# Causal attention and an ELU feed-forward on one core: new durations, and engines counted free ahead of an operation's end, in the plan that orders the instructions

## The chip, the core and the metric

The kernel runs on 1 core of one Trainium2 chip. The metric is device microseconds of one execution. The kernel before was run three times: 1034.64 us in the median, 1034.17 the fastest and 1037.37 the slowest.

## The reference

Eight batches of eight heads, 576 positions, head size 64; the bias of the scores is a cumulative sum along each head. Its output, 4608 tokens of 512, goes through a feed-forward with 2048 hidden units. All inputs are float32 except for the two weight matrices, which come as float64.

```
cum = np.cumsum(np.maximum(s, 0.0), axis=-1)
bias = -(cum[:, :, :, None] - cum[:, :, None, :])
scores = scale * np.matmul(q, k.transpose(0, 1, 3, 2))
scores = np.where(causal, -1000000000.0, scores + np.minimum(bias, 0.0))
attn = softmax(scores)
x = np.matmul(attn, v).transpose(0, 2, 1, 3).reshape(B * S, H * D)
h = x @ w_in
g = np.where(h > 0.0, h, np.exp(np.minimum(h, 0.0)) - 1.0)
return g @ w_out
```

## The kernel before

**Attention.** A unit is one head of one batch, or a pair of heads for the first 64 rows. `prepare` loads keys and queries (tiles stk, stq), rounds them to float32r (kh, qs; helper `rounded`, lines 400 to 410) and takes the rest that rounding left (k, q; helper `rest`, 421 to 427), so that a score is two matmuls: rounded by rounded, and the rests. `softmax_block` (1140 to 1165) makes the scores of a block of 128 rows on TensorE (line 1151, PSUM bank sc), adds the mask and finds the extreme of each row on VectorE (1154, tile mn), and takes the exponent with its sum on ScalarE (1159); 1163 and 1165 make the reciprocals of the sums. `halved` (1178 to 1215) splits the weighted probabilities into two float16 parts, high (1202 on GpSimd, 1204 on VectorE or 1206 on ScalarE) and low (1210 on VectorE, or 1196 and 1197, two instructions, on GpSimd), and a DMA transposes them into T. `weighing` (1262) multiplies them with the values (1324, bank av); `produce` (805) splits the result into the network's float16 input x. The first pairs ("low" units, lines 853 to 995, tiles kl, ql, pl, tl, avl) work in plain float32, with transposes on TensorE (947 and 968).

**Network.** The 4608 tokens are 18 chunks of 256. For each chunk and each pair of hidden blocks, `hidden` (1518) makes 24 float16 matmuls into a bank h (1539), five steps of the ELU on ScalarE and VectorE (1557, 1562 or 1566, 1570, 1574 or 1576, 1579, tiles g and gg), and `project` (1584) makes 2 x 6 matmuls into o (1600). The first chunk, and a part of the second, use float32 matmuls instead (1475 and 1505), because the weights' float16 parts are not ready.

**The plan.** Nothing of this is issued in program order. Each call of `op` registers an operation: a priority, one or more ways to do it (an engine, a cost in ns, a function that issues the instructions), and the tiles read and written. `Plan.issue` (178 to 288) then works like a list scheduler. It keeps a time `free` for each engine. In each step it computes for every operation whose inputs are planned when it could start: the latest of the engine's `free`, the end of its inputs plus a hop between engines (99 to 106), the time its buffers come free plus 150 ns, and, for the ways named DVE-SB and Pool, a port between VectorE and GpSimd, whose user's end less a lead is the other's earliest start. Among an operation's ways it takes the one with the earliest start plus cost, with VectorE's cost taken 1.3-fold (108, 109). It issues the operation with the earliest start, and of equals the one with the lower priority number: the network's steps beside TensorE have -1000, attention 0 to some 300, the network's matmuls 10000 and more. The planned order of each engine is the order in which it runs on the chip, and each engine waits at its next instruction until that one's inputs are there. Some switches go by the planned time of TensorE: the filler transposes (1663, 300 of them on offer) end at 60 us, one PSUM bank goes from the scores to the hidden layer at 165 us, and at 300 us the choice of certain buffers changes.

The costs are functions of the columns n: `pe`, `pe4`, `pe16` for TensorE, `act_c`, `act_s` for ScalarE, `dve_p`, `dve_b`, `dve_1`, `dve_2` for VectorE, `pool_1`, `pool_2` for GpSimd (291 to 341), or numbers in place. An operation can be several instructions.

Of the kernel before, what the change touches and what calls it, by code (L numbers as in the profile page):

```python
# [17 lines left out]
P = 128  # L18
# [70 lines left out]
class Plan:  # L89
# [20 lines left out]

    PORT_LEAD = {"DVE-SB": 240.0, "Pool": 120.0}

    ENGINE = {"DVE-SB": "DVE", "Pool-M": "Pool"}
# [64 lines left out]
    def issue(self):  # L178
# [19 lines left out]
        while pending:  # L198
# [56 lines left out]
            self.log.append((engine, start, end, o.prio))  # L255
            free[engine] = end
            for b, k in o.new:
# [33 lines left out]
def pe(n):  # L291

    return max(0.4525 * n, 111.0)


def pe4(n):

    return 4 * pe(n)

# [36 lines left out]
def pool_1(n):  # L336
    return 120 + 1.04 * n
# [7 lines left out]
def kernel(  # L345
# [66 lines left out]
    def scaled(prio, n, dst, src, by, reads, writes):  # L412

        op(prio, [
            ("Pool", 160 + 1.04 * n,
             lambda: pool.tensor_scalar(dst(), src(), by(), 1.0, ALU.mult, ALU.mult)),
            ("ACT", 295 + n / 1.2, lambda: act.activation(dst(), src(), AF.Copy, scale=by())),
            ("DVE-SB", 220 + 0.7 * n, lambda: dve.tensor_scalar(dst(), src(), by(), None, ALU.mult)),
        ], reads, writes)
# [52 lines left out]
    def clear_keys(k):  # L472

        return [("Pool-M", pool_1(2 * LOW), lambda: pool.memset(k()[HB:], 0.0))]

# [154 lines left out]
    def scales_of(prio, spans, dst):  # L630

        n = len(spans)
        tops = all_tops[n > 1 or dst == S_FIRST]
        bank = any_bank(f"peaks_{dst}")
        every = lambda: bank.v[:, P : P + n]
        own = plan.buf(sb, [P, 4], F32, f"own_{dst}", tag="own_first" if dst == S_FIRST else f"own{n}")

        def largest():
            for m, (at, k) in enumerate(spans):
                dve.tensor_reduce(tops.v[:, m : m + 1], peaks.v[:, at : at + k], mybir.AxisListType.X, ALU.max)  # L640

# [12 lines left out]
        op(prio, [("PE", pe4(P), lambda: pe_.matmul(every(), all_ones.v, own.v[:, :n], start=True, stop=True))],  # L654
           [all_ones, own], [bank])
        op(prio, [("DVE", 160.0, lambda: dve.tensor_copy(scales.v[:, dst : dst + n], every()))],
           [bank], [(scales, dst)])
# [208 lines left out]
    def prepare_low(u):  # L866
# [10 lines left out]
        load(prio, lambda: queries()[:HB], lambda: qT[b, j, :HB, : 2 * LOW], [], [key("q")], P * LOW * 4)  # L877
        op(prio if n else -10, [("Pool-M", pool_1(2 * LOW), lambda: pool.memset(queries()[HB:], 1.0))],
           [], [key("ones")])
# [58 lines left out]
    def weighing_low(u):  # L938
# [6 lines left out]
        def pair():  # L945
            tr = score_bank(f"trl_{u.tag}")
            op(prio, [("PE", 111.0, lambda: pe_.transpose(tr.v[:, :P], u.first.v, ident))], [u.first], [tr],
               late=[low_scale[u.b]] if u.b in low_scale else ())
            psum_copy(prio, P, lambda: turned.v[:, :P], lambda: tr.v[:, :P], [tr], [(turned, "pair")])

            def products():
                for h in range(2):
                    pe_.matmul(av.v[h * HB : (h + 1) * HB, :HB], u.vs_of()[:, 0], turned.v[:, h * HB : (h + 1) * HB],
                               start=True, stop=True)

            op(prio, [("PE", 2 * pe4(HB), products)], [(turned, "pair"), u.vs], [av])

        def keys(kb):
# [27 lines left out]

            op(prio, [("PE", pe4(c), products)], [(turned, kb), u.vs], [av])
            if kb < CUT:
# [151 lines left out]
    def softmax_block(prio, tag, native, pt, w, mask, mv, reads, operands, inv, view=lambda v: v):  # L1140
# [4 lines left out]
        for i in range(n):  # L1145
            sc = score_bank(f"sc_{tag}_{i}")

            def scores(i=i, sc=sc):
# [3 lines left out]

            op(prio, [("PE", pe4(cw) if native else 2 * pe(cw), scores)], reads, [sc])
            op(prio, [("DVE", 84 + dve_p(cw), lambda i=i, sc=sc: dve.tensor_tensor_reduce(  # L1154
                pt.v[:, i * cw : (i + 1) * cw], sc.v[:, :cw], mv(i * cw, cw), scale,
                BIG if i == 0 else mn.v[:, 0:1], ALU.add, ALU.min, mn.v[:, i : i + 1]))],
               [sc, mask], [(pt, "data"), mn])
        sm, col, last, ns, up = inv
        op(prio, [("ACT", 480 + w / 1.2, lambda: act.activation(  # L1159
            pt.v[:, :w], pt.v[:, :w], AF.Exp, bias=mn.v[:, n - 1 : n], scale=-1.0,  # L1160
            accum_out=sm.v[:, col : col + 1]))], [mn], [(pt, "data"), (sm, col)])
        if last:
            op(prio, [("ACT", 225.0, lambda: act.activation(
                sm.v[:, :ns], sm.v[:, :ns], AF.Relu, bias=EPS / up, scale=1.0 / up))], [], [sm])
            op(prio, [("DVE", 180.0, lambda: dve.reciprocal(sm.v[:, :ns], sm.v[:, :ns]))], [], [sm])  # L1165

    def normalize(prio, pt, w, sm, col):
        r = slice(col, col + 1)
        op(prio, [
            ("Pool", 160 + 1.04 * w, lambda: pool.tensor_scalar(  # L1170
                pt.v[:, :w], pt.v[:, :w], sm.v[:, r], 1.0, ALU.mult, ALU.mult)),
# [6 lines left out]
    def halved(u, i, pt, sm, col):  # L1178
# [20 lines left out]
        for part, n in ((whole, k * P), (rest, HB))[: 1 + (i == u.last)]:  # L1199
            high, low = (part, 0), (part, 1)  # L1200
            op(prio, [
                ("Pool", 160 + 1.04 * n, lambda part=part: pool.tensor_scalar(  # L1202
                    part(t16, 0), own(part), sm.v[:, r], 1.0, ALU.mult, ALU.mult)),
# [207 lines left out]
    def input_scale(ch, cs):  # L1411
# [7 lines left out]
        def steps():  # L1419
# [10 lines left out]

        op(side, [("DVE-SB", 80.0 + 160 * (len(cols) - 1), steps)],
           [(scales, c + m) for c in cols for m in range(2)], [(cs, "input")])
        if len(cols) == 1:
            return
        for m, (lo, up, _) in enumerate(parts):
            x, o = xs[lo // TX], lo % TX
            keys = [(part, *key) for a, e, _, key in x_parts[lo // TX] if a < up and e > lo for part in range(2)]
            op(side, [("DVE-SB", 100 + 0.55 * 8 * (up - lo), lambda x=x, o=o, n=up - lo, m=m: dve.tensor_scalar(
                x.v[:, :, :, o : o + n], x.v[:, :, :, o : o + n], cs.v[:, 1 + m : 2 + m], None, ALU.mult))],
               [(cs, "input")], [(x, key) for key in keys])  # L1440

    def group_constants(ch, cs):
# [4 lines left out]
        def steps():  # L1447
# [297 lines left out]
```

## Time and profile before

| | |
|---|---|
| median of three runs | 1034.64 us |
| the profiled execution | 1037.26 us, its span 1035.5 us, granted clock 1.00 |
| PE (TensorE) matmuls | 98% of the span |
| ScalarE (ACT) and GpSimd (POOL) | 616.0 and 418.0 us busy |
| float16 hidden matmuls, L1539 on x | 3072, 377.2 us |
| float16 output matmuls, L1600 | 1608, 380.7 us |
| moved by the DMA queues | 137.76 MB, 133 GB/s over the span |

The span goes from the first to the last instruction. PE stands for matmuls, PEld for weight loads, DVE for VectorE, SP for SyncE, which issues the DMAs. Matmuls are pipelined and their ends are modelled, so the time of a matmul is read best from the start of one to the start of the next. A row of a group gives the line, engine, operation, tiles out<-in, shapes and count, then the busy time and the mean ns of one, then the idle time of the engine just before them and what ended it. A row of waits gives who waited for whom, the us in total, the number of times and the longest.

### The profile page before, as it was taken

What the parts mean: (1) busy time and instruction counts of PE and PEld (TensorE: products, weight loads), DVE (VectorE), ACT (ScalarE), POOL (GpSimd) and SP (SyncE); (2) the same over time, 40 slices, a digit from 0 to 9 for tenths busy, and PEclk for the clock granted to TensorE, in tenths of its full rate; (3) what the DMA queues carried; (4) which work ended last, traced back from release to release, by engine and by line L of the source; (5) the groups of instructions that cost most, each with busy time, mean ns of one, the idle gap of its engine ahead of it and who ended that gap; (6) DMA issues with size and microseconds to landing.
All of it is one profiled execution on the core that took longest, in us unless ns stands there. A gap on an engine that the chain in (4) does not pass through costs nothing.

```text
span 1035.5 us, 21491 instructions
## 1 busy us (share of the span) xinstructions
PE 1010.8 (98%) x7181; PEld 697.0 (67%) x7181; DVE 848.1 (82%) x2119; ACT 616.0 (59%) x1452; POOL 418.0 (40%) x675
## 2 busy tenths in 40 slices
PE   8899999999999999999999999999999999999998
PEld 6666666666666666676666666666767676766665
DVE  6999899898788888888898888888889888884333
ACT  4787755656567556666566656666555555653232
POOL 5342335634445345555555445453343344330000
PEclk9999999999999999999999999999999999999999
DMA  8666356374667655667565866675766556642000
GB/s 207 218 219 197 114 167 133 87 171 104 147 126 151 160 117 119 145 155 173 112 143 121 184 120 144 129 176 117 152 131 165 119 134 133 140 95 52 1 21 21
DMA packets 277823, 137.76 MB, mean 133 GB/s; under 512 B 211768, under 2 KB 255056, under 8 KB 277712
## 3 DMA queue, kind: packets, MB, share of 16 engines
q1 hardware_dynamic: 277712, 136.39, 56.5%
q8 instruction: 57, 0.93, 0.4%
q14 instruction: 54, 0.44, 0.1%
HBM read 70.22 MB, written 9.88 MB: 77 GB/s over the span
## 4 chain that ended last, share of the span: by engine, by line
PE 82%; DVE 9%; DMA 4%; issue 2%; ACT 1%; SPq 1%; POOL 0%; DVEq 0%; POOLq 0%; ACTq 0%
PE o L1600 32%; PE h L1539 30%; PE sc L1151 9%; PE av L1324 6%; DVE p L1210 2%; DMA w_raw<-in_w_out_dram 2%; PE o L1505 1%; DMA vs<-in_vb_dram 1%; PE h L1475 1%; SPq L392 1%; DVE p L1154 1%; PE avl L984 1%; PE trl L968 1%; DMA q<-qs 1%; DVE peaks L616 1%
## 5 line engine op out<-in xcount | busy, mean ns | idle before, releaser
L1600 PE MATMUL o<-wp,gg 128*128 128x512 f16 x1608 | 380.7, 380 | 0.6 <-DVE gg L1579 0.6
L1539 PE MATMUL h<-x,wp 128*128 128x256 f16 x3072 | 377.2, 273 | 1.7 <-DVE gg L1579 1.7
L1539 PEld LDWEIGHTS <-wp 128*128 128x128 f16 x3216 | 301.3, 98 | 68.8 <-issue 9.6
L1600 PEld LDWEIGHTS <-gg 128*128 128x128 f16 x1608 | 150.3, 98 | 155.7 <-issue 6.0
L1159 ACT ACTIVATE p<-p,mn 128x192 f32<-128x192 f32 (+1 forms) x232 | 143.9, 621 | 55.9 <-DVE mn L1154 50.6
L1210 DVE SCALAR_TENSOR_TENSOR p<-p,sm,p 128x512 f16<-128x512 f32 (+3 forms) x240 | 171.8, 739 | 2.9 <-POOL p L1202 1.3
L1557 ACT ACTIVATE g<-h,cs 128x512 f32<-128x512 f32 x134 | 91.8, 685 | 122.9 <-PE h L1539 120.6
L1202 POOL TENSOR_SCALAR p<-p,sm 128x512 f16<-128x512 f32 (+3 forms) x124 | 79.4, 647 | 132.9 <-DVE sm L1165 85.4
L1574 ACT ACTIVATE gg<-h,wc 128x512 f16<-128x512 f32 x125 | 85.7, 685 | 71.6 <-DVE h L1570 70.3
L1154 DVE CUSTOM_DVE_ANT_0 p<-sc,maskw 128x192 f32<-128x192 f32 (+1 forms) x232 | 108.6, 480 | 16.8 <-PE sc L1151 14.8
L1579 DVE SCALAR_TENSOR_TENSOR gg<-h,wc,gg 128x512 f16<-128x512 f32 x134 | 99.8, 745 | 17.7 <-ACT gg L1574 16.9
L1151 PE MATMUL sc<-kh,qs 128*128 128x192 f32 (+2 forms) x272 | 109.8, 407 | 4.3 <-DVE mn L1154 4.1
L1570 DVE SCALAR_TENSOR_TENSOR h<-g,cs,h 128x512 f32<-128x512 f32 x134 | 100.7, 752 | 11.1 <-ACT g L1562 6.8
L1151 PE MATMUL sc<-k,q 128*128 128x192 f32 (+2 forms) x272 | 83.8, 311 | 1.8 <-issue 1.1
L1566 DVE TENSOR_SCALAR g<-g 128x512 f32<-128x512 f32 x76 | 36.1, 475 | 56.0 <-ACT g L1557 55.6
L1151 PEld LDWEIGHTS sc<-kh,qs 128*128 128x128 f32 x272 | 51.5, 189 | 23.1 <-DVE mn L1154 7.9
L1206 ACT ACTIVATE p<-p,sm 128x512 f16<-128x512 f32 (+3 forms) x97 | 55.8, 592 | 14.8 <-DVE sm L1165 13.3
L1324 PE MATMUL av<-T,v 128*64 128x256 f16 (+5 forms) x896 | 60.4, 286 | 0.0
L425 POOL TENSOR_TENSOR qs<-stq,qs 64x512 fp32r<-64x512 f32 (+1 forms) x44 | 49.4, 1122 | 26.4 <-ACT qs L406 11.7
L1151 PEld LDWEIGHTS sc<-k,q 128*128 128x128 f32 x272 | 51.8, 190 | 4.6 <-issue 1.3
L1324 PEld LDWEIGHTS <-v 128*64 128x64 f16 x896 | 39.9, 110 | 19.2 <-issue 8.9
L404 POOL TENSOR_SCALAR qs<-stq 128x512 fp32r<-128x512 f32 (+1 forms) x36 | 19.3, 536 | 79.8 <-PE sc L1151 65.0
(194 smaller groups left out, 1384.2 us busy)
## 6 DMA issues: line engine op xcount, KB each, us to landing
stk<-in_kT_dram SPq DMA_DIRECT2D x64, 288.0 KB
stq<-in_qT_dram SPq DMA_DIRECT2D x40, 256.0 KB
va<-in_vb_dram SPq DMA_DIRECT2D x32, 320.0 KB
w_raw<-in_w_in_dram SPq DMA_DIRECT2D x16, 512.0 KB
w_raw<-in_w_out_dram SPq DMA_DIRECT2D x16, 512.0 KB
out_dram<-ost SPq DMA_DIRECT2D x32, 256.0 KB
q<-qs SPq DMA_DIRECT2D x40, 128.0 KB
T<-p SPq DMA_TRANSPOSE x208
```

Source lines behind the costliest of these rows:

```text
L1151: pe_.matmul(view(sc.v[:, :cw]), l, r, start=n == 0, stop=n == len(pairs) - 1)
L1154: op(prio, [("DVE", 84 + dve_p(cw), lambda i=i, sc=sc: dve.tensor_tensor_reduce(pt.v[:, i * cw : (i + 1) * cw], sc.v[:, :cw], mv(i * cw, c ...
L1159: op(prio, [("ACT", 480 + w / 1.2, lambda: act.activation(pt.v[:, :w], pt.v[:, :w], AF.Exp, bias=mn.v[:, n - 1 : n], scale=-1.0, accum_out ...
L1202: ("Pool", 160 + 1.04 * n, lambda part=part: pool.tensor_scalar(part(t16, 0), own(part), sm.v[:, r], 1.0, ALU.mult, ALU.mult)),
L1210: ("DVE-SB", dve_2(n), lambda part=part: dve.scalar_tensor_tensor(part(t16, 1), own(part), sm.v[:, r], part(t16, 0), ALU.mult, ALU.subtract)),
L1324: pe_.matmul(av.v[w.h * HB : (w.h + 1) * HB, dst], w.values.v[:, w.h, kb, v], part(w, kb, m), start=n == 0, stop=n == len(order) - 1,)
L1539: pe_.matmul(hp.v[:, m], weight_part(f, 0, part)[1]()[:, c * P : (c + 1) * P], x.v[:, xx, c, o : o + TC], start=(c == 0 and i == 0), stop= ...
L1557: op(side, [("ACT", act_c(2 * TC) + 90, lambda: act.activation(gt.v, flat(hp.v), AF.Exp, scale=by(BACK)))], [hp, (cs[ch], g)], [gt])
L1570: op(side, [("DVE", dve_b(2 * TC), lambda: dve.scalar_tensor_tensor(flat(hp.v), gt.v, by(MINUS if sign[0] else FIRST), flat(hp.v), ALU.mul ...
L1574: ("ACT", act_c(2 * TC) + 90, lambda: act.activation(flat(gg.v[:, 0]), flat(hp.v), AF.Copy, scale=down())),
L1579: op(side, [("DVE", dve_b(2 * TC), lambda: dve.scalar_tensor_tensor(flat(gg.v[:, 1]), flat(hp.v), down(), flat(gg.v[:, 0]), ALU.mult, ALU. ...
L1600: pe_.matmul(acc[i].v, gg.v[:, a, m, i * P : (i + 1) * P], weight_part(2 * fp + m, 1, part)[1](), start=(first and m == 0 and k == 0), sto ...
```

## The change

Three things change, all of them in numbers that the plan uses; no instruction, tile or dependency does.

First, after an operation is planned, its engine is counted free 85 ns (VectorE) or 105 ns (ScalarE) ahead of the operation's end; those who read its result still wait for the end. Second, TensorE's costs: float32 matmuls go from 1.81 n to 1.675 n + 5 ns; the products of two heads, each on half of the array's columns, get a cost of their own, and a score of two float32r matmuls gets 85 ns more. Third, single costs of the other engines: the masked score 74 ns less, the exponent 90 ns less, GpSimd's scaling 235 + 0.9 n in place of 160 + 1.04 n, GpSimd's way for the low halves 420 ns more, its wide memsets less, and some runs of small steps on VectorE more.

```
+    OVERLAP = {"DVE": 85.0, "ACT": 105.0}
...
-            free[engine] = end
+            free[engine] = end - self.OVERLAP.get(engine, 0.0)
...
 def pe4(n):
-    return 4 * pe(n)
+    return 1.675 * n + 5
+def pe4_half(n):
+    return 200 + 1.1 * n
+def pe_score(n):
+    return 2 * pe(n) + 85
...
     scaled, normalize, halved (high):
-            ("Pool", 160 + 1.04 * n,
+            ("Pool", 235 + 0.9 * n,
...
     memsets of low units' keys and queries:
-        return [("Pool-M", pool_1(2 * LOW), lambda: pool.memset(k()[HB:], 0.0))]
+        return [("Pool-M", 120 + 0.72 * 2 * LOW, lambda: pool.memset(k()[HB:], 0.0))]
...
     scales_of:
-        op(prio, [("DVE", 600.0, exponents)], [bank], [own])
-        op(prio, [("PE", pe4(P), ...
+        op(prio, [("DVE", 840.0, exponents)], [bank], [own])
+        op(prio, [("PE", 145.0, ...
...
     weighing_low:
-            op(prio, [("PE", 2 * pe4(HB), products)], [(turned, "pair"), u.vs], [av])
+            op(prio, [("PE", pe4_half(HB), products)], [(turned, "pair"), u.vs], [av])
-            op(prio, [("PE", pe4(c), products)], [(turned, kb), u.vs], [av])
+            op(prio, [("PE", pe4_half(c), products)], [(turned, kb), u.vs], [av])
...
     softmax_block:
-            op(prio, [("PE", pe4(cw) if native else 2 * pe(cw), scores)], reads, [sc])
-            op(prio, [("DVE", 84 + dve_p(cw), ...
+            op(prio, [("PE", pe4(cw) if native else pe_score(cw), scores)], reads, [sc])
+            op(prio, [("DVE", 10 + dve_p(cw), ...
-        op(prio, [("ACT", 480 + w / 1.2, ...
+        op(prio, [("ACT", 390 + w / 1.2, ...
-            op(prio, [("ACT", 225.0, ...
-            op(prio, [("DVE", 180.0, ...
+            op(prio, [("ACT", 205.0, ...
+            op(prio, [("DVE", 170.0, ...
...
     halved (low):
-                ("Pool", pool_1(n) + pool_2(n), lambda part=part: scaled_rest(part)),
+                ("Pool", 420 + pool_1(n) + pool_2(n), lambda part=part: scaled_rest(part)),
...
     input_scale, group_constants:
-        op(side, [("DVE-SB", 80.0 + 160 * (len(cols) - 1), steps)],
+        op(side, [("DVE-SB", 80.0 + 360 * (len(cols) - 1), steps)],
-            op(side, [("DVE-SB", 100 + 0.55 * 8 * (up - lo), ...
+            op(side, [("DVE-SB", 100 + 0.27 * 8 * (up - lo), ...
-        op(-1000 + ch, [("DVE-SB", 450.0, steps)],
+        op(-1000 + ch, [("DVE-SB", 780.0, steps)],
```

More of the change, by code (lines that the diff above doesn't have):

```diff
@@ L652, in scales_of @@
            [tops], [bank])
-        op(prio, [("DVE", 600.0, exponents)], [bank], [own])
-        op(prio, [("PE", pe4(P), lambda: pe_.matmul(every(), all_ones.v, own.v[:, :n], start=True, stop=True))],
+        op(prio, [("DVE", 840.0, exponents)], [bank], [own])
+        op(prio, [("PE", 145.0, lambda: pe_.matmul(every(), all_ones.v, own.v[:, :n], start=True, stop=True))],
            [all_ones, own], [bank])
@@ L877, in prepare_low @@
         load(prio, lambda: queries()[:HB], lambda: qT[b, j, :HB, : 2 * LOW], [], [key("q")], P * LOW * 4)
-        op(prio if n else -10, [("Pool-M", pool_1(2 * LOW), lambda: pool.memset(queries()[HB:], 1.0))],
+        op(prio if n else -10, [("Pool-M", 120 + 0.72 * 2 * LOW, lambda: pool.memset(queries()[HB:], 1.0))],
            [], [key("ones")])
@@ L1151, in scores @@
                     pe_.matmul(view(sc.v[:, :cw]), l, r, start=n == 0, stop=n == len(pairs) - 1)
-            op(prio, [("PE", pe4(cw) if native else 2 * pe(cw), scores)], reads, [sc])
-            op(prio, [("DVE", 84 + dve_p(cw), lambda i=i, sc=sc: dve.tensor_tensor_reduce(
+            op(prio, [("PE", pe4(cw) if native else pe_score(cw), scores)], reads, [sc])
+            op(prio, [("DVE", 10 + dve_p(cw), lambda i=i, sc=sc: dve.tensor_tensor_reduce(
                 pt.v[:, i * cw : (i + 1) * cw], sc.v[:, :cw], mv(i * cw, cw), scale,
@@ L1158, in softmax_block @@
         sm, col, last, ns, up = inv
-        op(prio, [("ACT", 480 + w / 1.2, lambda: act.activation(
+        op(prio, [("ACT", 390 + w / 1.2, lambda: act.activation(
             pt.v[:, :w], pt.v[:, :w], AF.Exp, bias=mn.v[:, n - 1 : n], scale=-1.0,
@@ L1162, in softmax_block @@
         if last:
-            op(prio, [("ACT", 225.0, lambda: act.activation(
+            op(prio, [("ACT", 205.0, lambda: act.activation(
                 sm.v[:, :ns], sm.v[:, :ns], AF.Relu, bias=EPS / up, scale=1.0 / up))], [], [sm])
-            op(prio, [("DVE", 180.0, lambda: dve.reciprocal(sm.v[:, :ns], sm.v[:, :ns]))], [], [sm])
+            op(prio, [("DVE", 170.0, lambda: dve.reciprocal(sm.v[:, :ns], sm.v[:, :ns]))], [], [sm])
     def normalize(prio, pt, w, sm, col):
@@ L1169, in normalize @@
         op(prio, [
-            ("Pool", 160 + 1.04 * w, lambda: pool.tensor_scalar(
+            ("Pool", 235 + 0.9 * w, lambda: pool.tensor_scalar(
                 pt.v[:, :w], pt.v[:, :w], sm.v[:, r], 1.0, ALU.mult, ALU.mult)),
@@ L1201, in halved @@
             op(prio, [
-                ("Pool", 160 + 1.04 * n, lambda part=part: pool.tensor_scalar(
+                ("Pool", 235 + 0.9 * n, lambda part=part: pool.tensor_scalar(
                     part(t16, 0), own(part), sm.v[:, r], 1.0, ALU.mult, ALU.mult)),
@@ L1437, in input_scale @@
             keys = [(part, *key) for a, e, _, key in x_parts[lo // TX] if a < up and e > lo for part in range(2)]
-            op(side, [("DVE-SB", 100 + 0.55 * 8 * (up - lo), lambda x=x, o=o, n=up - lo, m=m: dve.tensor_scalar(
+            op(side, [("DVE-SB", 100 + 0.27 * 8 * (up - lo), lambda x=x, o=o, n=up - lo, m=m: dve.tensor_scalar(
                 x.v[:, :, :, o : o + n], x.v[:, :, :, o : o + n], cs.v[:, 1 + m : 2 + m], None, ALU.mult))],
```

## The prediction

> **What bounds the kernel.** I read the page's shares first, then the busy time by stage, then the chain of waits and the counts of matmuls inside the long stage, then single instructions in the order of time, and last what the PE waited for. The page's span and its two busiest engines:
>
> ```profile
> span 1035.5 us, 21491 instructions
> ...
> PE 1010.8 (98%) x7181; PEld 697.0 (67%) x7181; DVE 848.1 (82%) x2119; ACT 616.0 (59%) x1452; POOL 418.0 (40%) x675
> ```
>
> PE is idle for 1035.5 - 1010.8 = 24.7 us, and the ends of matmuls are modelled, so some more may be hidden. The windows by stage (busy us and instructions of PE, PEld, DVE, ACT and POOL, then the granted clock, the DMA share and GB/s) say where:
>
> ```profile
> 0.00:50.00 50.00, 42.44 (x269) 32.41 (x270) 37.61 (x104) 30.05 (x86) 22.68 (x66) 1.00 0.73 207
> 50.00:200.00 150.00, 142.42 (x789) 94.84 (x788) 137.75 (x375) 102.15 (x267) 63.34 (x108) 1.00 0.55 160
> 200.00:925.00 725.00, 719.61 (x5368) 498.33 (x5366) 628.89 (x1567) 446.87 (x1042) 328.76 (x496) 1.00 0.63 138
> 925.00:1036.00 111.00, 106.30 (x762) 71.44 (x760) 43.90 (x75) 36.94 (x60) 3.21 (x6) 1.00 0.12 27
> ```
>
> Idle time of PE: 50 - 42.44 = 7.6 us in the start, 150 - 142.42 = 7.6 us while the first chunks go through, 725 - 719.61 = 5.4 us in the long stage where attention and network run together, and some 4 us at the end (the window reaches 0.5 us past the span). DVE is busy for 137.75 / 150 = 92% of the second stage and 628.89 / 725 = 87% of the third.
>
> Is the PE of the long stage really full, or do modelled ends hide gaps? Three steps of the chain of waits give the pace of a full PE:
>
> ```profile
> 293.36 2.62 PE h L1539 x24
> 296.18 2.61 PE o L1600 x12
> ...
> 307.85 2.06 PE av L1324 x28
> ```
>
> The counts of the same stage, by line: first row L1539 (hidden layer), second L1600 (output projection), third L1324 (weighing of values), fourth L1151 (scores):
>
> ```profile
> 200.00:925.00 725.00, 325.99 (x2633) 244.92 (x2631) 1.00 0.63 138
> 200.00:925.00 725.00, 314.25 (x1320) 122.40 (x1320) 1.00 0.63 138
> 200.00:925.00 725.00, 55.26 (x812) 36.21 (x812) 1.00 0.63 138
> 200.00:925.00 725.00, 138.36 (x531) 86.42 (x531) 1.00 0.63 138
> ```
>
> 2633 x 2.62/24 = 287.4 us; 1320 x 2.61/12 = 287.1; 812 x 2.06/28 = 59.7. That is 634.2 us and leaves 90.8 us for 531 score matmuls, 0.34 us a pair; the pair in the next fence takes 0.35 us. So the stage is filled by matmuls as fast as they go. The same multiplications have to be made whatever the order, and no order can take more out of this stage than the few us of idle time.
>
> **What the plan counts, against what the trace shows.** The plan's numbers decide only order and which engine does a step; no instruction is made cheaper. So I first check whether the new numbers are the truer ones. Ten instructions in the order of time (start, duration, engine, line):
>
> ```profile
> 600.63 0.47 DVE L1210 SCALAR_TENSOR_TENSOR p<-p,sm,p 128x64 f16<-128x64 f32 x1
> ...
> 601.01 0.74 DVE L1570 SCALAR_TENSOR_TENSOR h<-g,cs,h 128x512 f32<-128x512 f32 x1
> ...
> 601.67 0.61 DVE L1154 CUSTOM_DVE_ANT_0 p<-sc,maskw 128x448 f32<-128x448 f32 x1
> ...
> 602.22 0.08 DVE L1154 DVE_READ_ACCUMULATOR2_ANT mn<- 128x1 f32 x1
> 602.22 0.45 DVE L1154 CUSTOM_DVE_ANT_0 p<-sc,maskw 128x288 f32<-128x288 f32 x1
> ...
> 602.38 0.66 ACT L1159 ACTIVATE p<-p,mn 128x448 f32<-128x448 f32 x1
> ...
> 602.81 0.38 PE L1151 MATMUL sc<-kh,qs 128*128 128x288 f32 x1
> ...
> 602.94 0.19 ACT L1159 ACTIVATION_READ_ACCUMULATOR p<-p,mn 128x1 f32 x1
> 603.03 0.29 PE L1151 MATMUL sc<-k,q 128*128 128x288 f32 x1
> ...
> 603.16 0.50 PE L1539 MATMUL h<-x,wp 128*128 128x256 f16 x3
> ```
>
> DVE, masked scores of 448 columns: from 601.67 to the start of the next at 602.22 is 0.55 us. Before, the plan holds DVE for 84 + 155 + 1.04 x 448 = 705 ns; after, for 10 + 155 + 466 - 85 = 546 ns. DVE, L1570: from 601.01 to 601.67 is 0.66 us; before 215 + 532 = 747 ns, after 662. The new numbers are right to 1% in both, and the second instruction starts 0.08 us ahead of the end of the first (601.01 + 0.74 = 601.75). ACT, exponent of 448 columns with its sum: from 602.38 to 603.13, 0.75 us; before 853 ns, after 763 to the result. PE, a score pair of 288 columns: 603.16 - 602.81 = 0.35 us; before 2 x 130 = 261 ns, after 346. So the old plan counted DVE as occupied longer than it is, by about 0.085 us for each of the long stage's 1567 DVE instructions, 133 us at most (those that read an accumulator belong to another step, so it is less), and PE's scores as shorter, by 531/2 x 0.085 = 22.6 us. By the old count DVE needs about 629 + 133 = 762 us of a stage of 725 and is its bound; by the new one it has room.
>
> The Trainium skill (VectorE: DVE Perf Modes, section "The DRAIN you can't avoid") says that the next DVE instruction does not start until the pipeline of the one ahead has emptied. By that rule the 85 ns would be a mistake, and the sum would have none of it; the rows at 601.01 and 601.67 overlap by 0.08 us, so the trace disagrees.
>
> **What it can bring, part by part.** The waits of PE in the second stage (the four longest), then all of them in the long stage:
>
> ```profile
> PE sc L1151 <- DVE mn L1154: 2.5, 3, 1.3
> PE trl L947 <- POOL pl L1170: 1.7, 3, 0.8
> PE tr_None L1277 <- ACT psh_None L1174: 1.2, 1, 1.2
> PE avl L953 <- DVE tl L432: 1.1, 1, 1.1
> ```
>
> ```profile
> PE sc L1151 <- DVE mn L1154: 1.8, 4, 0.7
> PE h L1539 <- DVE gg L1579: 1.7, 1, 1.7
> PE sc L1151 <- issue: 1.1, 1, 1.1
> PE o L1600 <- DVE gg L1579: 0.6, 1, 0.6
> ```
>
> Every one but the 1.1 us of "issue" is PE at a place in its fixed order that another engine had not reached: 2.5 + 1.7 + 1.2 + 1.1 = 6.5 us in the second stage, 1.8 + 1.7 + 0.6 = 4.1 us in the long one. A plan whose durations are right puts other PE work there. It cannot remove them all: with few chunks begun, the second stage has little other work, and in it DVE is nearly full. Bounds: from nothing to 10.6 us. I take half, 3.2 + 2.0 = 5.2 us, since no row favours either end.
>
> The start gets nothing in my sum. Its chain is made of loads:
>
> ```profile
> 4.63 5.38 DMA vs<-in_vb_dram
> 10.02 6.86 DMA vs<-in_vb_dram
> ```
>
> These and the weight loads behind them run at the 207 GB/s of the first window, and the plan's costs of SyncE's issues are not changed. A changed order there can bring or cost up to the 7.6 us of idle time.
>
> What moves to another engine: the lower halves that Pool makes in two instructions cost 420 ns more in the plan, so most of them should go to DVE. The rows of those with 64 columns, and of DVE's own at that size:
>
> ```profile
> L1196 POOL TENSOR_SCALAR p<-p,sm 128x64 f32<-128x64 f32 x25 | 13.0, 518 | 8.6 <-ACT p L1206 4.0 <-DVE p L1204 2.8
> L1197 POOL TENSOR_TENSOR p<-p,p 128x64 f16<-128x64 f32 x25 | 10.8, 433 | 2.1
> L1210 DVE SCALAR_TENSOR_TENSOR p<-p,sm,p 128x64 f16<-128x64 f32 x39 | 14.2, 363 | 0.5 <-ACT p L1206 0.2 <-POOL p L1202 0.2
> ```
>
> If all 25 move, Pool loses 13.0 + 10.8 = 23.8 us and DVE gains 25 x 0.363 = 9.1 us. In the long stage DVE has 725 - 629 = 96 us free, which covers it; if that cover were gone, the 9.1 us would be paid in full. In the second stage, 150 of the 875 us, its share is 9.1 x 150/875 = 1.6 us on a DVE that is nearly full: I count 1.4 us. With DVE and ACT counted free 85 and 105 ns earlier, other steps will lean from Pool to them too; nothing in the trace says how many, and I price them at nothing because the same 96 us and ACT's 725 - 447 = 278 us cover them. The shorter counts for memsets, reciprocals and native matmuls (80 hidden and 40 output multiplications) and the longer ones for Pool's scaling, exponents and constants only move places in the order; their own price is nothing.
>
> Sum: -5.2 + 1.4 = -3.8 us. The profiled execution took 1037.26 us around its span of 1035.5, at the upper end of the runs (1034.17 to 1037.37), so I take the change off the median: 1034.64 - 3.8 = **1030.8 us**; a profiled execution like this one would come out near a span of 1031.7.
>
> **The rivals.** First, no difference: the waits just listed are replaced by others of the same size, since a fixed order always meets some late step and the greedy choice has no goal but the earliest start; then 1034.6, give or take 3. For it speaks that 725 us are full already. To this belongs the case that the new numbers hardly alter any order, as attention's priorities decide: also 1034.6.
>
> Second, slower: PE loses a reserve that the wrong numbers gave it. Before, DVE ran ahead of its plan by 85 ns an instruction and PE behind by 85 ns a score pair, so DVE's results lay ready when PE came to them, and a late DVE instruction hit nobody. After, both are planned tightly, and DVE instructions are late at times for a reason that the plan holds only roughly, Pool on the same memory at once:
>
> ```profile
> 626.75 1.40 POOL L425 TENSOR_TENSOR k<-stk,kh 64x576 fp32r<-64x576 f32 x1
> ...
> 627.37 1.34 DVE L1210 SCALAR_TENSOR_TENSOR p<-p,sm,p 128x512 f16<-128x512 f32 x1
> ...
> 629.09 0.74 DVE L1210 SCALAR_TENSOR_TENSOR p<-p,sm,p 128x512 f16<-128x512 f32 x1
> ```
>
> ```profile
> L1210 DVE SCALAR_TENSOR_TENSOR p<-p,sm,p 128x512 f16<-128x512 f32 x127 | 109.7, 882 | 1.0 <-ACT p L1206 0.2
> ```
>
> 127 x (0.882 - 0.74) = 18.0 us of lateness in all. If a third of it reaches PE at the score banks, that is 6.0 us: 1040.6. It decides as soon as PE's waits for mn (1.8 us in the long stage) pass some 6 us, more than all that can be won there. Against it: only those 1.8 us reach PE now, with the same lateness, and Pool is to do less.
>
> Third, DVE could be free only at the end of each instruction, as the page cited has it. Then up to 133 us of DVE's time in the long stage would be missing from the new plan, DVE would need 762 us there and bound it: 37 us more, 1071.6. The overlapping rows speak against it.
>
> **How the numbers follow.** A measurement of this kernel can tell about 0.3%, 3.1 us, from no change: faster is below 1031.5, slower above 1037.7. The forecast gets 0.50; it reaches from nearly nothing to all 10.6 us plus a little from the start, and I put 0.40 of it below 1031.5 and 0.10 above. No difference gets 0.23, all within the bound. Slower gets 0.26 and the third rival 0.01. That is 0.40 faster, 0.33 the same, 0.27 slower. The range goes from 1022 (10.6 us of waits and 2 us in the start gone) to 1042 (a little over 40% of the 18.0 us arriving), and leaves out some 0.1 at each end. The likeliest sign's own range is 1022 to 1031.5.
>
> **What would show it.** Right: PE's idle time in 50 to 200 us falls from 7.6 to about 4, in the long stage from 5.4 to about 3; L1196 and L1197 all but vanish from Pool, and L1210 grows by about 25; Pool's 418.0 us fall by 20 or more, and DVE's 848.1 rise by about 9. Attention ends earlier than 925 us, since the plan believes DVE and ACT to be quicker, and the stretch of pure network at the end gets longer at the same pace of 2.62 and 2.61 us. Wrong: PE's waits for mn or gg in the long stage pass 6 us (second rival), or the start loses more than the later stages win, or the PE gaps of the second stage stay with other names (first rival).

## The result and the profile after

The changed kernel takes 1075.62 us in the median of 4 runs (1072.18 to 1078.64); the kernel before, run beside it, 1035.95. The ratio is 1.0383, 95% interval 1.0341 to 1.0424: slower, about 40 us, where a gain of 3.8 us was forecast. The page's span and shares:

```profile
span 1076.9 us, 21431 instructions
...
PE 1033.4 (96%) x7179; PEld 697.4 (65%) x7179; DVE 876.9 (81%) x2228; ACT 634.5 (59%) x1489; POOL 298.0 (28%) x467
```

The windows by stage, with the columns as before (PE, PEld, DVE, ACT, POOL):

```profile
0.00:50.00 50.00, 45.03 (x276) 33.88 (x277) 36.44 (x103) 30.83 (x93) 21.83 (x64) 0.97 0.71 205
50.00:200.00 150.00, 145.00 (x810) 96.01 (x809) 141.19 (x369) 104.33 (x263) 55.78 (x85) 1.00 0.55 158
200.00:925.00 725.00, 695.65 (x5072) 468.90 (x5071) 643.62 (x1670) 451.52 (x1062) 220.35 (x319) 1.00 0.65 139
925.00:1077.00 152.00, 147.68 (x1027) 98.62 (x1025) 55.67 (x88) 47.80 (x74) 0.00 (x0) 1.00 0.07 20
```

The first two stages got better: PE's idle time goes from 7.6 to 5.0 us in each. In the long stage it goes from 5.4 to 725 - 695.65 = 29.4 us, and DVE is still not full there, 643.62 of 725. The counts of that stage by line, in the order L1551 (hidden layer), L1612 (output projection), L1336 (values) and L1163 (scores):

```profile
200.00:925.00 725.00, 300.39 (x2417) 226.91 (x2418) 1.00 0.65 139
200.00:925.00 725.00, 284.47 (x1203) 112.03 (x1201) 1.00 0.65 139
200.00:925.00 725.00, 57.42 (x840) 37.92 (x840) 1.00 0.65 139
200.00:925.00 725.00, 137.45 (x540) 85.23 (x540) 1.00 0.65 139
```

At the pace of a full PE taken from the kernel before, these are 263.9 + 261.7 + 61.8 + 540/2 x 0.34 = 91.8, in all 679.2 us of matmuls. That is the count of what the kernel before fitted into 725 us, so PE stood still for some 46 us more of the stage than before; the windows, with modelled ends, show 24 of them (29.4 against 5.4). What was not done in the stage was done behind it. The hidden matmuls and the output matmuls after 925 us, first before, then after:

```profile
925.00:1036.00 111.00, 52.90 (x456) 44.46 (x456) 1.00 0.12 27
925.00:1036.00 111.00, 55.26 (x242) 23.34 (x240) 1.00 0.12 27
```

```profile
925.00:1077.00 152.00, 75.30 (x651) 63.44 (x649) 1.00 0.07 20
925.00:1077.00 152.00, 79.52 (x348) 33.97 (x348) 1.00 0.07 20
```

195 hidden and 106 output matmuls more are left for the end: 195 x 2.62/24 + 106 x 2.61/12 = 44.3 us, about the 41.4 us by which the span grew (some of the values' matmuls moved the other way). Attention itself ended sooner: its last score matmul starts at 923.03 us in place of 931.81, its last group of value matmuls at 935.66 in place of 945.39. What suffered is the network, which got less of PE beside it. The chain of work that ended last, first before, then after, now goes through VectorE (DVE) for three times the share:

```profile
PE 82%; DVE 9%; DMA 4%; issue 2%; ACT 1%; SPq 1%; POOL 0%; DVEq 0%; POOLq 0%; ACTq 0%
```

```profile
PE 54%; DVE 29%; issue 7%; ACT 4%; DMA 3%; SPq 1%; POOL 0%; DVEq 0%; ACTq 0%; POOLq 0%
```

Who held PE up in the long stage (waits in total, times, longest):

```profile
PE sc L1163 <- DVE mn L1166: 18.1, 31, 1.6
PE sc L1163 <- DVE pc_None L1232: 2.3, 2, 1.6
PE av_None L1282 <- DVE x L847: 2.0, 5, 1.1
PE o L1612 <- DVE gg L1591: 1.5, 4, 0.5
```

18.1 us at scores, whose bank VectorE has not yet read; it was 1.8. This is the second rival's mark, three times past its point of decision.

**What the plan believed.** `Plan.issue` knows the latest end that it planned (line 288 of the kernel before), and its log has the planned start and end of each operation. This is the plan's own arithmetic, done while the program is built, and no measurement, but beside a span it tells whether a loss was planned or came on the chip. TensorE's idle time in the plan is its planned last end less its planned work. "Release" stands for an engine that is counted free ahead of an operation's end; e1 to e17 are the experiments below.

| kernel | planned end, us | TensorE idle in the plan, us | span in the profile, us | span less planned end, us |
|---|---|---|---|---|
| before | 1028.5 | 8.1 | 1035.5 | 7.0 |
| after | 1024.4 | 5.0 | 1076.9 | 52.5 |
| e1, release alone | 1023.5 | 4.6 | 1058.1 | 34.6 |
| e2, without release | 1039.7 | 18.1 | 1048.2 | 8.5 |
| e3, ScalarE's release left | 1045.5 | 25.2 | 1053.5 | 8.0 |
| e4, old softmax costs | 1026.2 | 7.0 | 1053.3 | 27.1 |
| e5, SBUF operations 150 ns longer | 1036.1 | 15.8 | 1048.7 | 12.6 |
| e6, GpSimd's costs alone | 1026.1 | 7.7 | 1029.7 | 3.6 |
| e7, TensorE's costs alone | 1044.7 | 22.6 | 1042.8 | -1.9 |
| e8, more reserve | 1050.2 | 28.4 | 1051.1 | 0.9 |
| e9, ports apart | 1029.1 | 10.9 | 1056.4 | 27.3 |
| e10, half the release | 1026.4 | 5.9 | 1042.3 | 15.9 |
| e11, memset costs alone | 1024.4 | 4.4 | 1030.0 | 5.6 |
| e12, e6 and a small release | 1025.1 | 4.3 | 1030.8 | 5.7 |
| e13, e2 with TensorE's old costs | 1027.5 | 7.8 | 1033.4 | 5.9 |
| e14, score cost alone | 1050.3 | 5.1 | 1037.4 | -12.9 |
| e15, float32 costs alone | 1016.4 | 19.1 | 1033.5 | 17.1 |
| e16, memset cost lower | 1033.0 | 11.0 | 1039.6 | 6.6 |
| e17, GpSimd out of the choices | 1027.8 | 7.5 | 1053.7 | 25.9 |

The changed plan is the better one by its own count, by 4.1 us, and the chip falls 52.5 us behind it; before, it was 7.0. The last column sorts the runs: wherever VectorE has its whole release, the chip ends 12.6 to 52.5 us late, with half of it 15.9, and without it, or with e12's 15 ns, at most 8.5. Only e14 and e15 stand apart: before, two errors in TensorE's costs nearly cancel, and each of these runs corrects one of the two, so their plans hold 1044.0 and 996.0 us of TensorE's work where the others hold 1017 to 1021.

### The profile page after: what moved, and what is told of

Read it like the earlier page. It is cut to its first block, busy times and chain, and to the rows that moved or that the text cites. A ratio compares the mean times of both kernels' runs of the same rounds, so it can differ in the third digit from the quotient of the medians.

```text
span 1076.9 us, 21431 instructions
## 1 busy us (share of the span) xinstructions
PE 1033.4 (96%) x7179; PEld 697.4 (65%) x7179; DVE 876.9 (81%) x2228; ACT 634.5 (59%) x1489; POOL 298.0 (28%) x467
## 4 chain that ended last, share of the span: by engine, by line
PE 54%; DVE 29%; issue 7%; ACT 4%; DMA 3%; SPq 1%; POOL 0%; DVEq 0%; ACTq 0%; POOLq 0%
PE o L1612 19%; PE h L1551 18%; DVE p L1222 7%; PE sc L1163 7%; DVE p L1166 4%; PE av L1336 3%; DVE h L1582 2%; PE h L1487 2%; PE o L1517 2%; ACT p L1171 2%; DVE v L1043 1%; DVE gg L1591 1%; PE trl L980 1%; DVE x L847 1%; DVE qs L436 1%
## 5 line engine op out<-in xcount | busy, mean ns | idle before, releaser
L1612 PE MATMUL o<-wp,gg 128*128 128x512 f16 x1608 | 377.7, 380 | 2.5 <-DVE gg L1591 1.7
L1551 PE MATMUL h<-x,wp 128*128 128x256 f16 x3072 | 376.5, 274 | 0.0
L1551 PEld LDWEIGHTS <-wp 128*128 128x128 f16 x3216 | 304.6, 98 | 65.7 <-issue 7.1
L1612 PEld LDWEIGHTS <-gg 128*128 128x128 f16 x1608 | 151.5, 98 | 160.8 <-DVE gg L1591 5.3
L1222 DVE SCALAR_TENSOR_TENSOR p<-p,sm,p 128x512 f16<-128x512 f32 (+3 forms) x266 | 179.6, 701 | 2.0 <-POOL p L1214 0.6
L1586 ACT ACTIVATE gg<-h,wc 128x512 f16<-128x512 f32 x131 | 89.7, 685 | 95.3 <-DVE h L1582 94.4
L1163 PE MATMUL sc<-kh,qs 128*128 128x192 f32 (+2 forms) x272 | 109.0, 404 | 25.2 <-DVE mn L1166 21.9
L1591 DVE SCALAR_TENSOR_TENSOR gg<-h,wc,gg 128x512 f16<-128x512 f32 x134 | 99.9, 746 | 32.7 <-ACT gg L1586 32.0
L1214 POOL TENSOR_SCALAR p<-p,sm 128x512 f16<-128x512 f32 (+3 forms) x92 | 69.9, 765 | 199.1 <-DVE sm L1177 135.3
L1582 DVE SCALAR_TENSOR_TENSOR h<-g,cs,h 128x512 f32<-128x512 f32 x134 | 100.5, 750 | 6.9 <-ACT g L1574 2.4
L1163 PEld LDWEIGHTS sc<-kh,qs 128*128 128x128 f32 x272 | 51.2, 188 | 62.7 <-DVE mn L1166 35.8
L1163 PE MATMUL sc<-k,q 128*128 128x192 f32 (+2 forms) x272 | 83.7, 311 | 0.8 <-DMA q<-qs 0.8
L1218 ACT ACTIVATE p<-p,sm 128x512 f16<-128x512 f32 (+3 forms) x119 | 64.0, 560 | 13.0 <-DVE sm L1177 12.6
L1336 PE MATMUL av<-T,v 128*64 128x256 f16 (+5 forms) x896 | 61.0, 286 | 1.4 <-DMA T<-p 1.4
L1163 PEld LDWEIGHTS sc<-k,q 128*128 128x128 f32 x272 | 51.6, 190 | 3.1 <-DMA q<-qs 0.9
L1336 PEld LDWEIGHTS <-v 128*64 128x64 f16 x896 | 40.4, 110 | 19.8 <-issue 9.7
L437 POOL TENSOR_TENSOR k<-stk,kh 64x576 fp32r<-64x576 f32 x28 | 41.7, 1489 | 24.9 <-ACT kh L418 19.1
L1171 ACT ACTIVATION_READ_ACCUMULATOR p<-p,mn 128x1 f32 x232 | 43.6, 188 | 0.0
```

The costliest lines, as they stand in the source:

```text
L1163: pe_.matmul(view(sc.v[:, :cw]), l, r, start=n == 0, stop=n == len(pairs) - 1)
L1171: op(prio, [("ACT", 390 + w / 1.2, lambda: act.activation(pt.v[:, :w], pt.v[:, :w], AF.Exp, bias=mn.v[:, n - 1 : n], scale=-1.0, accum_out ...
L1214: ("Pool", 235 + 0.9 * n, lambda part=part: pool.tensor_scalar(part(t16, 0), own(part), sm.v[:, r], 1.0, ALU.mult, ALU.mult)),
L1222: ("DVE-SB", dve_2(n), lambda part=part: dve.scalar_tensor_tensor(part(t16, 1), own(part), sm.v[:, r], part(t16, 0), ALU.mult, ALU.subtract)),
L1336: pe_.matmul(av.v[w.h * HB : (w.h + 1) * HB, dst], w.values.v[:, w.h, kb, v], part(w, kb, m), start=n == 0, stop=n == len(order) - 1,)
L1551: pe_.matmul(hp.v[:, m], weight_part(f, 0, part)[1]()[:, c * P : (c + 1) * P], x.v[:, xx, c, o : o + TC], start=(c == 0 and i == 0), stop= ...
```

## The experiments

The theories: **A, the reserve.** The old durations were too long for VectorE, and this covered what the plan does not hold; the change takes this cover (time counted too long) away, VectorE falls behind, and PE, whose order is fixed, waits for it. **B, moved work.** The loss comes from the low halves that go from GpSimd to VectorE. **C, any new order costs this much.** Medians and ratios are to the kernel before on the same chip.

### e1 to e4: the early release and the softmax costs

e1 adds to the kernel before:

```
+    OVERLAP = {"DVE": 85.0, "ACT": 105.0}
...
-            free[engine] = end
+            free[engine] = end - self.OVERLAP.get(engine, 0.0)
```

> The kernel before with one part of the change: VectorE and ScalarE counted free 85 and 105 ns ahead of an operation's end, all costs as before. Theory A, the reserve: the old durations were on the whole too long, and this covered the waits and slowdowns that the plan does not hold; without it the chip falls behind the plan and TensorE waits at the score banks. Then this part, which takes some 85 ns from each of about 1600 VectorE operations, is the largest share of the loss: 20 us or more slower than before, 1055 to 1085 us. Theory B, moved work: the loss comes from the low halves that go from GpSimd to a nearly full VectorE because of the 420 ns. Then this kernel is within 6 us of before. Theory C, any new order costs this much: about 1076, with no one cause.

Measured: 1059.85 us, ratio 1.024 (1.0217 to 1.0263), 24 us more.

e2 sets `OVERLAP = {}` in the changed kernel, e3 `OVERLAP = {"ACT": 105.0}`.

> The changed kernel with the engines counted free at the operation's end again, all new costs kept. Theory A: most of the loss is gone, 1030 to 1050 us; VectorE's lateness is covered again but for the 74 ns taken from each masked score. Theory B: the low halves are still VectorE's, so about 1076. Theory C: 1060 to 1080.

> The changed kernel with VectorE counted free at the operation's end again, ScalarE still 105 ns ahead. Theory A, with VectorE as the engine that lags: as e2, 1030 to 1050 us. If ScalarE's reserve matters as much, about halfway, 1055. Theory B and C: about 1076.

Measured: e2 1050.61 us, 1.0157 (1.0132 to 1.0183); e3 1054.80 us, 1.0197 (1.0169 to 1.0224).

e4 puts the old softmax costs back into the changed kernel:

```
-            op(prio, [("DVE", 10 + dve_p(cw), ...
+            op(prio, [("DVE", 84 + dve_p(cw), ...
...
-        op(prio, [("ACT", 390 + w / 1.2, ...
+        op(prio, [("ACT", 480 + w / 1.2, ...
...
```

> The changed kernel with the old, longer costs of the masked score (74 ns), the exponent (90 ns), the sums (20 ns) and the reciprocal (10 ns). Theory A: about 352 x 74 ns = 26 us of VectorE's reserve come back, a quarter or a third of what was taken, so a third of the 40 us: 1055 to 1068. Theory B: about 1076. Theory C: anything from 1035 to 1080.

Measured: 1054.78 us, 1.0193 (1.0173 to 1.0213). The waits at the score banks in the long stage, of e1, e2 and e4 in this order:

```profile
PE sc L1153 <- DVE mn L1156: 12.1, 19, 1.4
```

```profile
PE sc L1163 <- DVE mn L1166: 7.2, 12, 1.5
```

```profile
PE sc L1163 <- DVE mn L1166: 11.7, 20, 1.3
```

The release alone gives more than half of the loss, and either kind of reserve put back takes away half of it or more (25 and 21 us), so the two overlap, as a reserve does that only has to be large enough. e4 lies just below what A expected (1055 to 1068). VectorE's release is the greater part: with ScalarE's alone left (e3) the time is 4 us above e2, and the chip is no further behind its plan (8.0 us) than in e2. B expected other numbers in all four and C in three; for e4 C allowed any number. But e2 keeps 15 us of loss, just past the upper edge of A (1050).

### e5 and e6: VectorE's lateness, and GpSimd's costs

e5 plans every VectorE operation on SBUF alone 150 ns longer, in the changed kernel:

```
+    LATE = {"DVE-SB": 150.0}
...
-            end = start + cost
+            end = start + cost + self.LATE.get(engine, 0.0)
```

> The changed kernel, with 150 ns added to the planned end of each VectorE operation that reads and writes SBUF alone and so meets GpSimd; the choice between engines goes by the changed costs as they are. In the changed kernel's trace such operations follow one another 100 to 180 ns later on average than planned (L1222, L436, L1043, L1216), while operations on PSUM are within 10 ns. Theory A, the reserve: this is the lateness itself, put where it arises, so half or more of the loss returns, 1036 to 1058 us. If it is not the mean but the spread that counts, a third at most: 1060 to 1068. Theory B, moved work (low halves from GpSimd to VectorE): about 1076, with VectorE as busy as before.

Measured: 1050.22 us, 1.0131 (1.0100 to 1.0163). PE's waits for mn in the long stage, and VectorE's low halves at 512 columns:

```profile
PE sc L1165 <- DVE mn L1168: 3.0, 7, 0.7
```

```profile
L1224 DVE SCALAR_TENSOR_TENSOR p<-p,sm,p 128x512 f16<-128x512 f32 x128 | 110.0, 873 | 2.9 <-POOL p L1216 1.2 <-ACT p L1220 0.8
```

The instructions did not get faster (873 ns; 834 in the changed kernel), but the plan now knows of them, and the waits for mn fall from 18.1 to 3.0 us. 25 of the 40 us return, with the early release in place, so the mean counts, not only the spread. That it must be these operations isn't shown by e5 alone: e2 and e4 put as much reserve back in other places. Two waits for gg, 4.9 us together, are now PE's largest in the stage.

e6 gives the kernel before the change's GpSimd costs alone:

```
-            ("Pool", 160 + 1.04 * n,
+            ("Pool", 235 + 0.9 * n,
...
-                ("Pool", pool_1(n) + pool_2(n), lambda part=part: scaled_rest(part)),
+                ("Pool", 420 + pool_1(n) + pool_2(n), lambda part=part: scaled_rest(part)),
...
-        return [("Pool-M", pool_1(2 * LOW), ...
+        return [("Pool-M", 120 + 0.72 * 2 * LOW, ...
...
```

> The kernel before with the changed costs of GpSimd alone, the 420 ns among them. Theory A: VectorE's reserve is untouched, so within 8 us of before, 1028 to 1044. Theory B: this is the cause of what is left without the early release (15 us): about 1050. Theory C, any new order costs: 1045 or more.

Measured: 1032.36 us, 0.9972 (0.9957 to 0.9987): 3 us faster. B falls, and so does C in its plain form.

### e7 and e8: TensorE's costs alone, and more reserve

e7 gives the kernel before `pe4`, `pe4_half`, `pe_score` and the 145 ns of the change; e8 gives the kernel before `OVERLAP = {"DVE": -60.0}` and nothing else, so that VectorE counts as free 60 ns late.

> The kernel before with the changed costs of TensorE alone. Each score counts 85 ns longer, so TensorE's plan is longer by some 20 us, and the other engines keep their reserve. Theory A: more reserve for VectorE against TensorE, so no loss: 1028 to 1040 us. Theory C: 1045 or more.

> The kernel before with VectorE counted free 60 ns behind the end of each operation, the opposite of the change. Theory A: TensorE is full already in the long stage, so more reserve brings little there, 0 to 6 us faster (1029 to 1036); if the plan then starves the network of its input, it is slower by 5 to 15 us, but with waits at x or gg and not at the score banks. Theory C: 1045 or more, as any new order.

Measured: e7 1044.77 us, 1.0084 (1.0061 to 1.0107), a miss for A, which expected no loss. e8 1050.71 us, 1.0135 (1.0108 to 1.0163), the far end of what A allowed. The last window of e8:

```profile
925.00:1080.00 155.00, 121.89 (x898) 82.48 (x896) 67.77 (x136) 53.21 (x100) 22.65 (x34) 1.00 0.22 49
```

GpSimd is still at work after 925 us, which in the kernel before had 3.21 us left: attention itself was planned too slowly. In both kernels the span is within 2 us of the planned end. These losses were planned: the plan itself leaves TensorE idle for 22.6 and 28.4 us, 8.1 before. With VectorE counted too long and PE rightly (e7), or VectorE longer still (e8), the plan holds PE back, so too much reserve can cost as too little does. C's forecast for both, 1045 or more, comes out in e8 and almost in e7; against C stand e6 and, below, e11, e12 and e15, new orders that lose nothing.

### e9 to e12: the port, half a release, and single costs

e9 sets both leads of `PORT_LEAD` to 0 in the changed kernel; e10 halves e1's release; e11 is the memsets' line of e6 alone (both memsets); e12 is e6 with `OVERLAP = {"DVE": 15.0, "ACT": 30.0}`.

> The changed kernel, in which the plan lets an operation of VectorE on SBUF and one of GpSimd no more overlap (both leads 0 in place of 240 and 120 ns). If VectorE's lateness behind the plan comes from GpSimd on the same memory at once, L1222 at 512 columns goes from 834 ns on average towards the undisturbed 740 to 780, and a good part of the loss returns: 1040 to 1062 us. If the lateness comes from something else (waits on ScalarE, hops), L1222 gets shorter and the time stays at 1070 to 1080.

> The kernel before with half of the early release, 42.5 ns for VectorE and 52.5 for ScalarE. Whole, it cost 24 us. Theory A, the reserve, has a point from which the loss sets in, since TensorE was full before: between 1036 and 1050 us, and fewer waits for mn than the 12.1 us in the long stage of the whole release. If the size of the release doesn't matter (any new order): 1055 or more.

> The kernel before with the changed cost of the two wide memsets alone (24 of them, in the first 120 us). GpSimd's changed costs together brought 3 us. If the start is what they improve, this has most of it: 1030 to 1034 us; if it is the choice of engines later on, this stays at 1034 to 1037.

> GpSimd's changed costs as in e6, and a small early release, 15 ns for VectorE and 30 for ScalarE. Theory A: the reserve that covers VectorE's lateness is about as large as it must be (its planned and real times agree within some us before), so any release costs a little: 1032 to 1040 us, not faster than e6. If the reserve was larger than needed, 1028 to 1032.

Measured: e9 1060.61 us, 1.0242 (1.0214 to 1.0269); e10 1042.88, 1.0070 (1.0047 to 1.0094); e11 1030.22, 0.9953 (0.9939 to 0.9967); e12 1033.44, 0.9979 (0.9966 to 0.9992). In e9 the time moved as expected, but only in part for the expected reason: L1222 at 512 columns is still at 826 ns, while at 384 it falls from 755 to 618:

```profile
L1222 DVE SCALAR_TENSOR_TENSOR p<-p,sm,p 128x384 f16<-128x384 f32 x40 | 24.7, 618 | 0.0
```

The rest may be, again, time put into the plan, whose end is 4.7 us later. In e10 half the release costs 7 us and the whole 24, as a loss does that sets in when the cover is used up; one point between is no proof of it. The waits for mn of e10:

```profile
PE sc L1153 <- DVE mn L1156: 5.2, 7, 1.3
```

e11 is the fastest kernel of the study, faster than both; e12 is not faster than e6, as A expected.

### e13 to e16: what is left, and one cost at two values

e13 is e2 with TensorE's old costs; e14 is the kernel before with the 85 ns of a score alone, e15 with TensorE's float32 costs alone; e16 is e11 with 0.6 in place of 0.72.

> The changed kernel without the early release and with TensorE's old costs; what is left of the change are the costs of the other engines. Without the early release alone it took 1050.6 us, 15 more than before, and TensorE's costs alone cost 9. Theory A with two separate losses (VectorE's reserve; TensorE's costs): the 9 us go, 1038 to 1044. If the two losses are one and the same, nothing changes: 1048 to 1053. If TensorE's undercounted scores are themselves part of the reserve, the other way from what I held, up to 1060.

> The kernel before, with 85 ns more for each score pair and nothing else. TensorE's plan gets 25 us longer; if the plan then holds TensorE back against engines that it counts too long as well, the loss of e7 is here: 1042 to 1050 us. If the loss of e7 came from the float32 costs of the start: 1033 to 1038.

> The kernel before with TensorE's changed float32 costs alone, without the scores' 85 ns; they count only in the first 200 us, by about 25 us in all. If the plan of the start is what they spoil: 1040 to 1046 us. If the scores are the cause of e7's loss: 1030 to 1038.

> The kernel before with the two wide memsets at 120 + 0.6 ns a column, 504 ns, where the trace has 625 and e11 had 581. If e11's 5 us come from the truer number, this lies between: 1030 to 1036 us. If they are the luck of one order among many, this can come out on the other side, 1036 to 1042.

Measured: e13 1037.12 us, 1.0023 (1.0004 to 1.0041); e14 1041.37, 1.0061 (1.0041 to 1.0082); e15 1033.82, 0.9994 (0.9982 to 1.0006); e16 1042.50, 1.0071 (1.0056 to 1.0086). So the 15 us that e2 kept go with TensorE's costs, 13 of them, and the plan has this loss too: it leaves TensorE idle for 18.1 us in e2 and 7.8 in e13. Taken off in this order, the early release is worth 25 us, TensorE's costs 13.5 and all other costs 2.5; that these add up is no test, as each is the step from one run to the next. The changed kernel's own plan has only 5.0 us of idle time, so its loss is all lateness behind the plan. e14 and e15 put most of e7's 9 us at the scores' 85 ns, but this is not firm: e14's plan has no such idle time (5.1 us), and 6.8 us is within what e16 shows next.

e16 sets a bound to what single steps mean. Two values of one cost, 504 and 581 ns for a memset that takes 626 or more, give 1042.5 and 1030.2 us, and the kernel before, which counts 786, lies between. One late step does part of it; e16's wait of PE in the long stage:

```profile
PE h L1539 <- DVE x L1438: 3.1, 1, 3.1
```

So 5 to 8 us either way can be what one order has over another, and e11's gain may be that order's and not the truer number's. The losses of e7, e10 and e14 (9, 7 and 7 us) are of this size as well; those of the other slower runs (14.5 us and more) are not.

### e17: GpSimd out of the choices

The changed kernel, with one line in `op`:

```
+        ways = [w for w in ways if w[0] != "Pool" or len(ways) == 1]
```

> The changed kernel, in which GpSimd keeps only the steps that no other engine can do (memsets, masks); VectorE and ScalarE take the rest. If GpSimd on SBUF at once is what makes VectorE's SBUF operations late, L1222 at 512 columns goes from 834 ns on average to the undisturbed 740 to 755, and TensorE's waits for mn fall well below 18 us though VectorE has more to do: 1035 to 1062 us. If the lateness is of another kind, L1222 stays above 800 and the time at 1065 or more. Were VectorE itself to become the bound, it would show above 95% busy in the long stage.

Measured: 1056.21 us, 1.0187 (1.0154 to 1.0219). The low halves of the changed kernel, then of e17:

```profile
L1222 DVE SCALAR_TENSOR_TENSOR p<-p,sm,p 128x512 f16<-128x512 f32 x128 | 104.0, 834 | 1.1 <-POOL p L1214 0.6
L1222 DVE SCALAR_TENSOR_TENSOR p<-p,sm,p 128x384 f16<-128x384 f32 x40 | 30.2, 755 | 0.0
L1222 DVE SCALAR_TENSOR_TENSOR p<-p,sm,p 128x256 f16<-128x256 f32 x40 | 25.5, 637 | 0.6
L1222 DVE SCALAR_TENSOR_TENSOR p<-p,sm,p 128x64 f16<-128x64 f32 x58 | 24.1, 415 | 0.2
```

```profile
L1223 DVE SCALAR_TENSOR_TENSOR p<-p,sm,p 128x512 f16<-128x512 f32 x128 | 92.2, 746 | 0.5
L1223 DVE SCALAR_TENSOR_TENSOR p<-p,sm,p 128x384 f16<-128x384 f32 x40 | 24.5, 612 | 0.0
L1223 DVE SCALAR_TENSOR_TENSOR p<-p,sm,p 128x256 f16<-128x256 f32 x40 | 19.1, 478 | 0.0
L1223 DVE SCALAR_TENSOR_TENSOR p<-p,sm,p 128x64 f16<-128x64 f32 x64 | 17.9, 280 | 0.4
```

Its long stage, and its wait for mn there:

```profile
200.00:925.00 725.00, 710.77 (x5180) 480.94 (x5178) 666.31 (x1831) 502.27 (x1194) 0.00 (x0) 1.00 0.64 139
```

```profile
PE sc L1164 <- DVE mn L1167: 8.9, 21, 1.1
```

Every size gets faster, by 88 to 159 ns, as soon as GpSimd is silent. VectorE does more (666.31 us in place of 643.62) and still PE waits half as long for mn, and half of the loss is gone. Part of VectorE's lateness is therefore GpSimd on the same memory; the rest is not, since 20 us remain and the chip still ends 25.9 us behind its plan.

## Why the prediction was wrong

**What bounds the kernel:** right. The long stage was full of matmuls before, and no order was going to win much there.

**The new numbers are the truer ones:** this step failed. I compared them with single rows, an instruction that nothing disturbed, and called them right to 1%. That holds for the masked scores, L1570 and the exponents. It does not hold for the mean of the steps on SBUF. The plan counts `dve_2(n)` = 160 + 1.06 n for a low half: 703, 567, 431 and 228 ns at 512, 384, 256 and 64 columns. The missing rows of the kernel before:

```profile
L1210 DVE SCALAR_TENSOR_TENSOR p<-p,sm,p 128x384 f16<-128x384 f32 x37 | 27.2, 736 | 0.0
L1210 DVE SCALAR_TENSOR_TENSOR p<-p,sm,p 128x256 f16<-128x256 f32 x37 | 24.0, 648 | 1.5 <-POOL p L1202 1.1
```

Before, they took longer than planned by 127 x 179 + 37 x 169 + 37 x 217 + 39 x 135 ns = 42.3 us; after, by 128 x 131 + 40 x 188 + 40 x 206 + 58 x 187 = 43.4. The lateness is the same. The cover is not: before, each of 352 masked scores was counted about 155 ns too long (705 against 550 at 448 columns), 54.6 us, and most other VectorE operations 85; after, nothing. In e17 the same sum is 128 x 43 + 40 x 45 + 40 x 47 + 64 x 52 = 12.5 us, and in e9, whose 256 and 64 columns are at 604 and 368 ns, 32.8.

**A sum that was wrong besides:** VectorE's 762 us by the old count. The 629 us of the stage are reported durations, and these already run some 85 ns into the next instruction; the old plan counted just so (L1570: 747 ns planned, 0.74 us reported). The 133 us lie inside the 629 and can't be added. The old plan's own log has 660.2 us of VectorE's operations between 200 and 925 us, so VectorE was not its bound there.

**The gain of 5.2 us from PE's waits:** partly right. The forecast of 3.8 us in all is near the 4.1 us by which the plan itself got shorter; what the chip makes of the plan was the part mis-priced. In the second stage, which was to fall from 7.6 to about 4, the idle time fell to 5.0. In the long stage it rose.

**The 9.1 us that go to VectorE:** right for the step, too small for the whole. L1222 has 266 instructions where L1210 had 240, as forecast. But of the other steps, which I priced at nothing because VectorE had 96 us free, far more moved: GpSimd fell by 120 us, not by some 24, and VectorE rose by 28.8. e1 shows much of it without GpSimd's changed costs (340.9 us on GpSimd), and e2 little without the release (389.2), so it is for the most part the early release that draws them. That free time covers such work is not refuted; e17 moves still more and is faster.

**The second rival:** right in mechanism, place and mark, wrong in size and chance. Its price, a third of 18.0 us, took one instruction's lateness at one size and let it reach PE once. In place of its 6.0 us, the waits for mn are 18.1 us, and PE stood still for some 46 us more of the long stage. My own figure said that the old plan counted up to 133 us too much for VectorE in the long stage; I took this as error to be removed, when it was what the plan lived on. Removing it put the whole plan ahead of what VectorE does, in every step anew, and the lateness added up.

**The range:** its upper end, 1042, rested on two fifths of the same 18.0 us. No rival held a loss of 40 us but the third one, which the overlapping rows excluded rightly; its 37 us came from the wrong 762, and that 1071.6 lies near the result is chance. The Trainium skill (VectorE: DVE Perf Modes, section "The DRAIN you can't avoid") adds, in the paragraph that the prediction drew on, that a next instruction that is not held starts earlier, so the rows do not go against the page.

**A sign that came true without its gain:** attention ended some 9 us sooner and the stretch of pure network at the end got longer, as forecast, but because matmuls had been put off.

**Left out altogether:** that PE's scores, counted 85 ns too short, also were part of a balance. I priced the longer cost at nothing; without the early release, TensorE's costs are worth 13.5 us (e13 against e2), and this loss is made in the plan, as idle time of TensorE. The changed kernel's plan has no such idle time (5.0 us), so what these costs do there is not shown.

**What stays open:** of the 20 us that e17 still loses, how much is each small shortfall, such as the 43 to 52 ns of the low halves even undisturbed, was not separated.

## What to carry to other kernels

In a fixed order across engines, a planned duration is also a reserve: count in it the mean time that an instruction holds its engine in the running kernel, neighbours included, and not the undisturbed one alone, or a true correction can take cover away. No run here did this in full; e5, the nearest, is still 14.5 us slower than the kernel before, so this is advice and not a result. What the runs do show is how to tell the two losses apart: compare the plan's own end with the trace's span. A span far behind the plan lacks reserve on some engine, and a span that meets a long plan, with idle time of the bounding engine in it, has too much, provided that this engine's own costs are right (e14 and e15 show what happens where they are not). A single number moved this kernel by 5 to 8 us either way, so judge a rule for such numbers by several orders, not by one.

## What the runs showed of the hardware

VectorE's two-input step on SBUF (128x512, float16 out) takes 746 ns in e17, where GpSimd is silent from 200 us on, and 807 to 891 on average in the other kernels, where GpSimd works beside it; single ones take 1.34 us. At 64 columns it is 280 against 415 ns in the changed kernel. The steps of the ELU that touch PSUM (L1582 and L1591, 128x512) do not change: 750 and 746 ns in the changed kernel, 752 and 746 in e17.

The Trainium skill (SBUF — State Buffer, section "SBUF: two separate sides") says that the ports shared by GpSimd and VectorE are an exclusive lock: an instruction of VectorE with two SBUF inputs and a GpSimd one that reads SBUF never run together, and the later one waits for the whole of the other. The trace agrees in kind and not to the letter: the step at 627.37 us, quoted in the prediction, was on until 628.71, 0.56 us behind GpSimd's, which was on from 626.75 to 628.15; the same step takes 0.74 us undisturbed, so a wait to GpSimd's reported end is not shown. The plan holds this lock by its planned times (`PORT_LEAD`), but the steps come at other times on the chip, and e9 shows that a wider berth in the plan keeps the two apart only in part.
